# Where a block of fused linear attention and two expert layers begins and ends: tiles kept, units made and products ordered anew

## The chip, the cores and the metric

The kernel runs on one core of a Trainium2 chip. Its time is the device time of one execution in microseconds (us). A core has a matrix engine (TensorE, PE in the profile), a vector engine (VectorE, DVE), a scalar engine (ScalarE, ACT), a general engine (GpSimd, POOL) and a sync engine (SyncE, SP), which here issues nearly all loads and stores. Each engine runs its own instructions in the order in which the program gives them; semaphores tie the engines together.

## What is computed

Three layers follow one another; all are in float32.

```python
# 1: linear attention with decay, 4 batches, 8 heads, 768 steps, head size 64
state = gamma[None, :, None, None] * state + einsum('bhd,bhe->bhde', k[:, :, t], v[:, :, t])
y[:, :, t] = scale * einsum('bhd,bhde->bhe', q[:, :, t], state)
# 2: gated layer on x, 3072 tokens x 512, d_ff = 1536
x = ((x @ w_a) * (x @ w_b)) @ w_out
# 3: eight experts, each token goes to the one with the largest logit, F = 1024
e_idx = argmax(x @ w_gate, axis=1)
gate_w = softmax(x @ w_gate)[arange(N), e_idx]
eom = sigmoid(x @ w_output_gate)
for e in range(8):
    mask = e_idx == e
    out[mask] = gate_w[mask, None] * eom[mask, e, None] * (relu(x[mask] @ w1[e]) @ w2[e])
```

## The kernel before

**Matmuls.** Each float32 product is three matmuls: `mm3` (lines 111 to 113) multiplies high by high, high by low and low by high parts. A tile is therefore split: ACT makes the high part (a cast), DVE the low part (the difference). A split of a 128x1024 tile is `L687` on ACT and `L688` on DVE; `L682` makes the difference of two quarters of x ahead of a split (`less`).

**Blocks of tokens.** The 3072 tokens are worked in four blocks: block 0 and block 1 with 512 tokens, block 2 and block 3 with 1024. In each, d_ff is walked in 12 steps f of 128 columns. Blocks 0 and 1 do it plainly: `proj`, `gate` (rows `gs`, cast on ACT and subtracted on DVE, lines 581 and 584), and `down`, which multiplies the gated rows with a w_out tile `wos` into the four banks acc0 to acc3.

**Blocks of sums.** Blocks 2 and 3 use a scheme with seven products in place of eight (`block_of_sums`). x is split into quarters and sums of them: B21, B11, U1, U2, B22, U3, U4. The weights of a step come as two `unit` tiles, the first with four and the second with three combinations of weight quarters. A step is seven `product` calls of six matmuls each, into two banks by turns: p1 (`r`) and p0 (`q`). Between the products ACT and DVE copy, add and multiply the banks into `a1`, `b2` and `g2`. `a1` becomes the gated rows `gs` of half of the tokens, used in the next step's `down`; `g2` is kept in `later` tiles for the other half. In block 2 (`fresh`) the units are made on the go: `load_weights` and `sum_weights` (four POOL sums, line 645) and `make_unit`, which loads the quarters kept in memory (`q_d`), casts on ACT (line 656) and subtracts on DVE (line 657); `store_unit` writes them to `q_d`, and block 3 loads them back with `load_unit`.

**Deferred passes.** `later_pass` runs after each of these blocks ("2d" after block 2, "3d" after block 3). It walks f again and multiplies the kept rows (`later_split`: `gd`) with w_out into four more banks. Its w_out tiles are loaded anew: `passes` is the list of (pass, f) in order, and `next_wos` issues the next load into a ring of three buffers. `between` finishes the block's last `down` and copies its banks out (`evac_x2`, lines 604 and 606).

**What runs beside.** `spread` deals other work out over the slots of a block: the attention of block j+1, the routing (`route`), the splitting of x (`x_steps`, which returns a list in two parts), and the loads of the experts. Expert 0's first rows (`up2`, `down2`) start right behind pass 3d: they are gathered (POOL, line 848) by an index table that `route` writes to memory by scatter (line 415), and a last part of the routing (`todo`) is dealt out over their loop. `load_expert` splits an expert's weights (ACT line 462, DVE line 463) and loads the next.

**Buffers.** `room(i, ...)` hands out one of some fourteen large buffers by number; a tile that takes a number waits until the last tile there has been read to its end. SP issues its DMAs in the order of the program: one that must wait for a buffer holds up those behind it.

Of the kernel before, what the change touches and what calls it, by code (L numbers as in the profile page):

```python
# [34 lines left out]
LEAD = 256  # L35
# [17 lines left out]
def attention_moe_moe2(ctx: ExitStack, tc: tile.TileContext, a: dict, out: bass.AP):  # L53
# [243 lines left out]
    def route(i0, n, by_pe):  # L297
# [134 lines left out]
        if by_pe:  # L432
            out = [bank((s_t, 0))]
            for t in range(1, n):
                out.append(bank((s_t, t), (s_l, t - 1)))
            return out + [bank((s_l, n - 1)), s_m, bank((s_r,)), lambda: (s_e(), s_s())]
# [109 lines left out]
    passes = [(j, f) for j in (2, "2d", 3, "3d") for f in range(NF1)]  # L546
# [76 lines left out]
    UNIT_AT = [7, XH, XL]  # L623
# [12 lines left out]
    def load_weights(f):  # L636
        if f < NF1:
            w = raw_w[f] = room(10, [128, 8, 256], F32, "wsum")
# [8 lines left out]
    def make_unit(n):  # L647

        if n < 2 * NF1:
            f, h = divmod(n, 2)  # L650
            t = new_unit(2, n)
            k = 1 if h else 2
            q0 = UNIT_Q[h][0]
            sync.dma_start(f32(t[:, :k]), q_d[f][:, q0 : q0 + k])
# [19 lines left out]
    def x_steps(j):  # L674
# [9 lines left out]
        def split(eng, q):  # L684
# [13 lines left out]
            split(dve, "U2"),  # L698
            split(dve, "U3"),
            less(dve, "U4", "B21", "U2"),  # L700
            split(dve, "B22"),
# [17 lines left out]
    LATER_AT = [8, 9, 11]  # L719

    def block_of_sums(j, slot):
        fresh = j == 2
        for f in range(NF1):
            next_wos()
# [26 lines left out]
            if fresh:  # L751
                low0 = make_unit(2 * f + 2)
# [28 lines left out]
            gt[j, f] = gs  # L781
            if fresh:
# [4 lines left out]
        return gd0  # L787
# [7 lines left out]
    def later_pass(j, gd, slot, between):  # L795

        key = f"{j}d"
        nxt = None
        for f in range(NF1):
            if 0 < f < NF1 - 1:  # L800
                next_wos()
            w = wos[key, f]
            for i, tag in enumerate(("p1", "p0", "acc0", "acc1")):
                if f == 0 and i == 2:
                    between()
                if i == 2 and f + 1 < NF1:
                    nxt = later_split(f + 1)
                if f == 0:
                    accs[4 + i] = sum_bank(tag)
                c = slice(128 * i, 128 * i + 128)  # L810
                mm3(accs[4 + i], gd[:, 0, c], gd[:, 1, c], w[:, 0], w[:, 1], f == 0, f == NF1 - 1)
            wos.pop((key, f))
            gd = nxt
            slot()

# [61 lines left out]
    def up(p, f, d, c0, n):  # L877
        cc = slice(c0, c0 + n)
        for k in range(KD):
# [3 lines left out]
    def up2(f, d, c0, n, which=None):  # L883
        up(ph[f % 2 if which is None else which], f, d, c0, n)
# [9 lines left out]

# [441 lines left out]
```

## Time and profile before

| what | value |
|---|---|
| median of 3 runs | 1042.28 us (1037.99 to 1044.7) |
| the profiled execution | 1038.58 us |
| its span | 1036.8 us |
| mean granted clock of TensorE | 0.987 of full speed |
| TensorE (PE) | 94% busy, 7248 matmuls |
| VectorE (DVE), ScalarE (ACT), GpSimd (POOL) | 59%, 35%, 24% busy |
| moved by DMA | 222.30 MB, mean 214 GB/s |
| w_out tiles | 48 loads of 512 KB |
| first units of a step from `q_d` (block 3) | 12 loads of 1024 KB |

The span is what the profiler saw from the first to the last instruction; the execution's own time is 1.8 us longer. Times in the rows below count from the start of the span. "Busy" of PE includes matmuls that wait inside the pipeline, so a full share need not be full speed.

Block 1's last steps and block 2's first lie between 259 and 297.6 us, the rest of block 2 up to 455, pass 2d up to 495.7, block 3 up to 650.6, pass 3d with the start of expert 0 up to 705.5, and the loop over expert 0's first rows up to 744.2. The experts behind that are not touched.

### The profile page before, as it was taken

What the parts mean: (1) busy time and instruction counts of PE and PEld (TensorE: products, weight loads), DVE (VectorE), ACT (ScalarE), POOL (GpSimd) and SP (SyncE); (2) the same over time, 40 slices, a digit from 0 to 9 for tenths busy, and PEclk for the clock granted to TensorE, in tenths of its full rate; (3) what the DMA queues carried; (4) which work ended last, traced back from release to release, by engine and by line L of the source; (5) the groups of instructions that cost most, each with busy time, mean ns of one, the idle gap of its engine ahead of it and who ended that gap; (6) DMA issues with size and microseconds to landing.
All of it is one profiled execution on the core that took longest, in us unless ns stands there. A gap on an engine that the chain in (4) does not pass through costs nothing. (4 is left out here: it accounts for less than half of the span.)

```text
span 1036.8 us, 19417 instructions
## 1 busy us (share of the span) xinstructions
PE 975.3 (94%) x7248; PEld 795.3 (77%) x7249; DVE 607.6 (59%) x1213; ACT 361.1 (35%) x668; POOL 249.6 (24%) x238
## 2 busy tenths in 40 slices
PE   6899999999779999989999999888799999999997
PEld 5688888877557777767777777667698888889886
DVE  4899866877627676555576576343265444444541
ACT  3677742223312222233211112333154443344431
POOL 3211011225415443520012212220420220311211
PEclk9899999999989999999999999999999999999999
DMA  6999968767876876656966864752374653535620
GB/s 240 345 330 313 295 216 314 271 239 194 298 300 245 283 233 208 249 144 225 351 218 223 265 218 158 226 201 61 104 215 152 192 173 101 169 114 185 192 90 28
DMA packets 78549, 222.30 MB, mean 214 GB/s; under 512 B 13374, under 2 KB 22846, under 8 KB 76865
## 3 DMA queue, kind: packets, MB, share of 16 engines
q1 hardware_dynamic: 71136, 201.06, 58.5%
q0 software_dynamic: 6704, 18.93, 5.4%
q8 instruction: 82, 1.34, 0.5%
q10 hardware_dynamic: 576, 0.56, 0.2%
q14 instruction: 51, 0.41, 0.1%
HBM read 170.13 MB, written 51.30 MB: 214 GB/s over the span
## 5 line engine op out<-in xcount | busy, mean ns | idle before, releaser
L922 DVE TENSOR_TENSOR ew<-wraw,ew 128x512 fp32r<-128x512 f32 x112 | 76.4, 690 | 55.6 <-ACT ew L921 49.0
L342 DVE SCALAR_TENSOR_TENSOR junkd<-x2r,wcol 128x512 bf16<-128x512 f32 x128 | 104.5, 816 | 3.6 <-DMA x2r<-x_d 1.5
L888 DVE SCALAR_TENSOR_TENSOR hs<-ph,hs 128x384 fp32r<-128x384 f32 (+4 forms) x72 | 39.0, 542 | 113.1 <-ACT hs L887 90.1
L111 PE MATMUL ph<-xe,ew 128*128 128x384 f32 (+4 forms) x288 | 98.1, 341 | 2.8 <-DVE x L604 2.1
L112 PE MATMUL ph<-xe,ew 128*128 128x384 f32 (+4 forms) x288 | 95.2, 330 | 0.3 <-DVE xe L873 0.3
L113 PE MATMUL ph<-xe,ew 128*128 128x384 f32 (+4 forms) x288 | 95.2, 330 | 0.0
L921 ACT CAST ew<-wraw 128x512 fp32r<-128x512 f32 x112 | 68.1, 617 | 57.7 <-PE acc L113 43.8
L111 PE MATMUL acc<-ew,hs 128*128 128x512 f32 (+1 forms) x216 | 85.6, 396 | 1.0 <-ACT hs L887 0.6
L113 PE MATMUL acc<-ew,hs 128*128 128x512 f32 (+1 forms) x216 | 85.5, 396 | 0.0
L112 PE MATMUL acc<-ew,hs 128*128 128x512 f32 (+1 forms) x216 | 85.3, 395 | 0.0
L111 PE MATMUL acc<-wos,gs 128*128 128x512 f32 x192 | 78.4, 408 | 6.2 <-ACT gs L779 4.8
L908 POOL DMA_INDIRECT out<-y,idx x27 | 27.5, 1018 | 230.6 <-ACT y L907 148.0
L765 POOL TENSOR_TENSOR later<-later,b 128x512 f32<-128x512 f32 x24 | 38.3, 1595 | 181.0 <-DVE b L764 181.0
L111 PE MATMUL p<-xs,ar 128*128 128x512 f32 x192 | 77.7, 405 | 1.4 <-DVE z L253 1.4
L111 PE MATMUL p<-U,unit 128*128 128x512 f32 x192 | 76.4, 398 | 2.4 <-DVE b L764 1.9
L113 PE MATMUL acc<-wos,gs 128*128 128x512 f32 x192 | 77.2, 402 | 0.8 <-DVE gs L780 0.8
L887 ACT ACTIVATE hs<-ph 128x384 fp32r<-128x384 f32 (+4 forms) x72 | 34.6, 480 | 122.1 <-PE ph L113 94.5
L113 PE MATMUL p<-xs,ar 128*128 128x512 f32 x192 | 75.7, 394 | 0.1
L112 PE MATMUL p<-xs,ar 128*128 128x512 f32 x192 | 75.6, 394 | 0.0
L112 PE MATMUL acc<-wos,gs 128*128 128x512 f32 x192 | 75.0, 390 | 0.0
L113 PE MATMUL p<-U,unit 128*128 128x512 f32 x192 | 74.8, 390 | 0.0
L112 PE MATMUL p<-U,unit 128*128 128x512 f32 x192 | 74.8, 390 | 0.0
(193 smaller groups left out, 2154.3 us busy)
## 6 DMA issues: line engine op xcount, KB each, us to landing
wraw<-in_ex SPq DMA_DIRECT2D x64, 512.0 KB
wos<-wos_d SPq DMA_DIRECT2D x48, 512.0 KB
wide<-in_w_ab SPq DMA_DIRECT2D x24, 512.0 KB
q_d<-unit SPq DMA_DIRECT2D x24, 512.0 KB
unit<-q_d SPq DMA_DIRECT2D x12, 1024.0 KB
qk<-in_qk SPq DMA_DIRECT2D x23, 512.0 KB
vk<-in_vk SPq DMA_DIRECT2D x23, 512.0 KB
q_d<-ar SPq DMA_DIRECT2D x36, 256.0 KB
```

Source lines behind the costliest of these rows:

```text
L111: pe.matmul(outp, lhsT=wh, rhs=rh, start=start, stop=False, skip_group_check=more)
L112: pe.matmul(outp, lhsT=wh, rhs=rl, start=False, stop=False, skip_group_check=more)
L113: pe.matmul(outp, lhsT=wl, rhs=rh, start=False, stop=stop, skip_group_check=more)
L342: dve.scalar_tensor_tensor(junk, x, 1.0, y, op0=ALU.mult, op1=ALU.mult, accum_out=out)
L765: pool.tensor_tensor(g2, g2, b2, op=ALU.mult)
L887: act.activation(h[:, 0, :n], p[:, :n], AF.Relu)
L888: dve.scalar_tensor_tensor(h[:, 1, :n], p[:, :n], 0.0, f32(h[:, 0, :n]), op0=ALU.max, op1=ALU.subtract)
L908: st = pool.indirect_dma_start(out=out[:, :], out_offset=bass.IndirectOffsetOnAxis(ap=ix[:, 1:2], axis=0), in_=y, in_offset=None, bounds_c ...
L921: act.copy(ew[f][:, part, 0], t[:, part])
L922: dve.tensor_tensor(ew[f][:, part, 1], t[:, part], f32(ew[f][:, part, 0]), op=ALU.subtract)
```

## The change

Five things are changed.

1. *w_out.* The tiles of f = 9, 10, 11 stay on chip at the end of block 2 and block 3, and the deferred pass begins with them (`KEPT`, `LATER_ORDER`). Pass 2d ends with f = 0, 1, 2, and block 3 begins with those three. `passes` is shorter by nine loads. The pass writes to p1, p0, acc2, acc3, and `between` finishes the row groups 2, 3 before 0, 1. In a block's last step the groups 2 and 3 of f = 10 come behind U4, and the first `later_split` ahead of U4.
2. *Units.* A unit's load (`fetch_unit`) is apart from its making. Unit 0 is asked for two steps earlier, unit 1 one step, the weights of f = 0 half a step, and the quarters are stored two steps earlier (`keep_quarters(f + 2)`). In block 2 the fetches come right behind the copy of a1 and behind U2.
3. *Splits of x for block 2.* Three steps come behind gate 11, two behind `make_unit(1)`, and four in the first slots of block 2, where attention then starts four slots later. B22 is split ahead of U3. The units of block 3 are loaded within pass 2d.
4. *Order in a step.* Product B11 stands ahead of `down(j, f - 1, [0])`.
5. *Expert 0's first rows.* `up2` is cut in two halves, and the routing's steps come three to an f. Four of the eight `load_expert` go from pass 3d into the ends of that loop's steps; banks change names.

The core of the diff:

```diff
+    KEPT = [NF1 - 3, NF1 - 2, NF1 - 1]
+    LATER_ORDER = {2: [*KEPT, *range(3, NF1 - 3), 0, 1, 2], 3: [*KEPT, *range(NF1 - 3)]}
-    passes = [(j, f) for j in (2, "2d", 3, "3d") for f in range(NF1)]
+    passes = [(2, f) for f in range(NF1)] + [("2d", f) for f in LATER_ORDER[2][3:]]
+    passes += [(3, f) for f in range(3, NF1)] + [("3d", f) for f in LATER_ORDER[3][3:]]
...
-    UNIT_AT = [7, XH, XL]
+    UNIT_AT = [7, 8, XH]
...
+    def fetch_unit(n):
+        if n < 2 * NF1:
+            f, h = divmod(n, 2)
+            k = 1 if h else 2
+            q0 = UNIT_Q[h][0]
+            sync.dma_start(f32(new_unit(2, n)[:, :k]), q_d[f][:, q0 : q0 + k])
...
 (block_of_sums)
-            next_wos()
+            last = f == NF1 - 1
+            if not last and (fresh or f > 1):
+                next_wos()
...
             act.copy(a1, r)
             if fresh:
+                fetch_unit(2 * f + 2)
                 sum_weights(f + 1)
             slot()
+            product(q, u, 0, "B11", True)
+            dve.tensor_tensor(a1, a1, q, op=ALU.add)
             if f:
                 down(j, f - 1, [0])
-            product(q, u, 0, "B11", True)
-            dve.tensor_tensor(a1, a1, q, op=ALU.add)
...
             if fresh:
+                fetch_unit(2 * f + 3)
                 low0 = make_unit(2 * f + 2)
...
-            if f:
+            if f and not last:
                 down(j, f - 1, [2, 3])
-                wos.pop((j, f - 1))
-            if f == NF1 - 1:
-                next_wos()
-                gd0 = later_split(0)
+            if last:
+                gd = later_split(KEPT[0])
             product(q, u, 0, "U4", False)
...
+            if last:
+                down(j, f - 1, [2, 3])
...
 (later_pass)
-            if 0 < f < NF1 - 1:
+            if 0 < n < NF1 - 2:
                 next_wos()
...
 (block 1)
+                    if f == 9:
+                        fetch_unit(0)
+                    if f == 10:
+                        load_weights(0)
+                        fetch_unit(1)
                     load_wo(f + 1)
-                    keep_quarters(f)
+                    if f + 2 < NF1:
+                        keep_quarters(f + 2)
...
-                        make_unit(1)()
-                        load_weights(1)
+                        for s in x_rest[:3]:
+                            s()
...
+                        make_unit(1)()
+                        for s in x_rest[3:5]:
+                            s()
...
-        slot, flush = spread([(attention_steps(3), 0, 78), (route(4, 4, False), 2, 82)])
+        slot, flush = spread([(x_rest[5:], 0, 4), (attention_steps(3), 4, 78), (route(4, 4, False), 14, 82)])
...
-        loads = [lambda f=f: load_expert(f) for f in range(6)]
+        loads = [lambda f=f: load_expert(f) for f in range(4)]
...
 (loop over expert 0's first rows)
-                up2(f, xst(0), LEAD, LEAD)
+                up2(f, xst(0), LEAD, LEAD, ks=range(2))
+                next_todo()
+                up2(f, xst(0), LEAD, LEAD, ks=range(2, KD))
                 hs[f] = relu(f, LEAD)
-                if todo:
-                    todo.pop(0)()
+                next_todo()
...
+            load_expert(f + 4)
```

**DVE, from the last steps of block 1 into block 2.** A row is a line of the code, the operation, what it writes and reads, and the size; `U1` to `U4`, `B11`, `B22` are split tails of x, `xraw` rows are differences ahead of a split, `g_sb` and `gs` are the gate of block 1, `unit` is a unit's tail. Before:

```order
L688 TENSOR_TENSOR B11_3300<-xraw_2001,B11_3300 128x1024
L682 TENSOR_TENSOR xraw_2001<-xraw_2671,xraw_2001 128x1024
L682 TENSOR_TENSOR xraw_2671<-xraw_2671 128x1024
L576 TENSOR_TENSOR g_sb_3341<-p1_3328,a_sb_3322 128x512
L584 TENSOR_TENSOR gs_3343<-g_sb_3341,gs_3343 128x512
L688 TENSOR_TENSOR U1_3348<-xraw_2001,U1_3348 128x1024
L682 TENSOR_TENSOR xraw_2001<-xraw_2671,xraw_2001 128x1024
L688 TENSOR_TENSOR U2_3364<-xraw_2001,U2_3364 128x1024
L688 TENSOR_TENSOR U3_3392<-xraw_2671,U3_3392 128x1024
L576 TENSOR_TENSOR g_sb_3408<-p1_3395,a_sb_3384 128x512
L584 TENSOR_TENSOR gs_3410<-g_sb_3408,gs_3410 128x512
L657 TENSOR_TENSOR unit_3413<-wsum_3346,unit_3413 128x2x256
```

With the change, from behind the gate of f = 10 on (`x2` is a copy out of block 1's first bank):

```order
L665 TENSOR_TENSOR unit_3175<-wsum_3311,unit_3175 128x2x256
L579 TENSOR_TENSOR g_sb_3403<-p1_3390,a_sb_3383 128x512
L587 TENSOR_TENSOR gs_3405<-g_sb_3403,gs_3405 128x512
L690 TENSOR_TENSOR xraw_2007<-xraw_2677,xraw_2007 128x1024
L690 TENSOR_TENSOR xraw_2677<-xraw_2677 128x1024
L696 TENSOR_TENSOR U1_3412<-xraw_2007,U1_3412 128x1024
L665 TENSOR_TENSOR unit_3313<-wsum_3311,unit_3313 128x2x256
L690 TENSOR_TENSOR xraw_2007<-xraw_2677,xraw_2007 128x1024
L696 TENSOR_TENSOR U2_3430<-xraw_2007,U2_3430 128x1024
L607 COPY x2_3450<-acc0_2155 128x512
L696 TENSOR_TENSOR B22_3481<-xraw_2677,B22_3481 128x1024
```

The tails of U1, U2 and U3 stood among the last gates of block 1 and now stand behind the last gate (the `gs` row), with those of B22 and U4 among and behind them; the tail of unit 0 stands ahead of that gate.

**PE, one step of block 3.** `p1` and `p0` are the two banks, `acc0` the first row group of `down`; the rows left out are more matmuls of the product above them. Before:

```order
L113 MATMUL p0_6450<-U4_5538,unit_6402 128x512
...
L113 MATMUL p1_6542<-B21_5346,unit_6443 128x512
L111 MATMUL acc0_5666<-wos_6351,gs_6533 128x512
L112 MATMUL acc0_5666<-wos_6351,gs_6533 128x512
L113 MATMUL acc0_5666<-wos_6351,gs_6533 128x512
L111 MATMUL p0_6543<-B11_5366,unit_6443 128x512
...
L113 MATMUL p0_6543<-B11_5366,unit_6443 128x512
L111 MATMUL p1_6542<-U1_5422,unit_6443 128x512
```

With the change:

```order
L113 MATMUL p0_6434<-U4_5534,unit_6384 128x512
...
L113 MATMUL p1_6528<-B21_5338,unit_6427 128x512
L111 MATMUL p0_6529<-B11_5358,unit_6427 128x512
...
L113 MATMUL p0_6529<-B11_5358,unit_6427 128x512
L111 MATMUL acc0_5655<-wos_6335,gs_6519 128x512
L112 MATMUL acc0_5655<-wos_6335,gs_6519 128x512
L113 MATMUL acc0_5655<-wos_6335,gs_6519 128x512
L111 MATMUL p1_6528<-U1_5416,unit_6427 128x512
```

The six matmuls of B11 have moved from behind the three of `acc0` to the place ahead of them, right behind B21.

**SP's queue, from the end of block 2 through pass 2d.** `wos` is a w_out tile, `unit` a unit for block 3, `x_d<-x` a store of finished rows (three more of them where rows are left out). Before:

```order
L552 DMA wos<-wos_d 128x1024
L634 DMA unit<-q_d 128x2048
L552 DMA wos<-wos_d 128x1024
L610 DMA x_d<-x_5323 128x512
...
L552 DMA wos<-wos_d 128x1024 x10
L634 DMA unit<-q_d 128x1536
L634 DMA unit<-q_d 128x2048
L610 DMA x_d<-x_5557 128x512
```

With the change:

```order
L673 DMA q_d<-unit 128x1024 x2
L613 DMA x_d<-x_5315 128x512
...
L555 DMA wos<-wos_d 128x1024 x2
L637 DMA unit<-q_d 128x2048
L555 DMA wos<-wos_d 128x1024 x3
L637 DMA unit<-q_d 128x1536
L555 DMA wos<-wos_d 128x1024 x3
L637 DMA unit<-q_d 128x2048
L555 DMA wos<-wos_d 128x1024
L613 DMA x_d<-x_5549 128x512
```

Two w_out tiles and a unit stood ahead of the first stores and ten tiles behind them; now the stores come first, nine tiles follow, and three units stand among them.

## Rows read from the trace of the kernel before

**Rows 1.** The page, part 1: busy time, share of the span, instructions.
```profile
PE 975.3 (94%) x7248; PEld 795.3 (77%) x7249; DVE 607.6 (59%) x1213; ACT 361.1 (35%) x668; POOL 249.6 (24%) x238
```

**Rows 2.** Stretches (us): busy time and count per engine, PE clock, DMA share, GB/s.
```profile
259.00:297.60 38.60, 24.57 (x203) 17.68 (x202) 16.70 (x24) 10.89 (x19) 13.44 (x15) 0.87 0.89 326
297.60:455.00 157.40, 154.82 (x1423) 120.58 (x1422) 101.42 (x214) 40.33 (x79) 71.39 (x68) 1.00 0.67 229
455.00:495.70 40.70, 36.47 (x158) 28.91 (x157) 24.59 (x27) 16.28 (x23) 2.24 (x2) 1.00 0.72 232
495.70:650.60 154.90, 151.04 (x642) 117.52 (x641) 99.58 (x242) 29.11 (x53) 31.77 (x25) 1.00 0.68 231
650.60:705.50 54.90, 45.60 (x217) 35.81 (x216) 22.64 (x47) 19.78 (x35) 10.12 (x10) 0.97 0.68 212
705.50:744.20 38.70, 31.61 (x206) 27.84 (x206) 10.42 (x37) 9.13 (x23) 5.90 (x6) 0.96 0.23 63
```

**Rows 3.** PE's timeline, 290 to 293: start, length, instruction, [idle before <-releaser].
```profile
292.67 0.79 PE L111 MATMUL p<-B,unit 128*128 128x512 f32 x1 [10.50 <-DMA unit<-q_d]
```

**Rows 4.** DVE by line, 252 to 284: group | busy, mean ns | idle before.
```profile
L688 DVE TENSOR_TENSOR U<-xraw,U 128x1024 fp32r<-128x1024 f32 x4 | 5.2, 1295 | 1.8 <-ACT U L687 1.8
...
L682 DVE TENSOR_TENSOR xraw<-xraw 128x1024 f32<-128x1024 f32 x2 | 2.4, 1218 | 0.0
```

**Rows 5.** ACT by line, 252 to 284.
```profile
L687 ACT CAST U<-xraw 128x1024 fp32r<-128x1024 f32 x4 | 4.2, 1050 | 5.0 <-DVE xraw L682 5.0
```

**Rows 6.** DVE's timeline, 255 to 284.
```profile
262.85 0.69 DVE L584 TENSOR_TENSOR gs<-g_sb,gs 128x512 fp32r<-128x512 f32 x1 [0.68 <-ACT gs L581]
...
277.45 1.75 DVE L657 TENSOR_TENSOR unit<-wsum,unit 128x512 fp32r<-128x512 f32 x1
```

**Rows 7.** POOL by line, 252 to 284.
```profile
L645 POOL TENSOR_TENSOR wsum<-wsum 128x256 f32<-128x256 f32 x8 | 6.2, 792 | 10.8 <-DMA wsum<-wab_d 10.6
```

**Rows 8.** Stretches right behind two waits of PE, columns as in rows 2.
```profile
292.60:297.60 5.00, 4.93 (x15) 3.96 (x16) 0.00 (x0) 0.59 (x1) 1.57 (x3) 0.70 0.95 384
668.20:671.00 2.80, 2.72 (x7) 2.17 (x8) 0.00 (x0) 0.00 (x0) 0.00 (x0) 0.50 0.76 310
```

**Rows 9.** PE's timeline in a step of block 3.
```profile
597.63 0.39 PE L113 MATMUL p<-U,unit 128*128 128x512 f32 x1
...
598.99 0.39 PE L113 MATMUL p<-B,unit 128*128 128x512 f32 x1
599.70 0.50 PE L111 MATMUL acc<-wos,gs 128*128 128x512 f32 x1 [0.32 <-ACT gs L779]
...
600.76 0.39 PE L111 MATMUL p<-B,unit 128*128 128x512 f32 x1
```

**Rows 10.** All engines' timeline in the same step: ACT and DVE.
```profile
599.02 0.62 ACT L779 CAST gs<-a 128x512 fp32r<-128x512 f32 x1 [5.82 <-DVE a L777]
599.67 0.69 DVE L780 TENSOR_TENSOR gs<-a,gs 128x512 fp32r<-128x512 f32 x1 [0.68 <-ACT gs L779]
...
600.45 0.59 ACT L732 COPY a<-p 128x512 f32<-128x512 f32 x1 [0.81 <-DVE gs L780]
```

**Rows 11.** PE's waits in block 2's rest, then block 3: us, times, longest.
```profile
PE acc L111 <- ACT gs L779: 2.1, 4, 0.5
...
PE acc L111 <- ACT gs L779: 2.7, 7, 0.8
```

**Rows 12.** PE's waits in pass 2d, then pass 3d.
```profile
PE p L111 <- DMA wos<-wos_d: 3.6, 2, 2.7
...
PE p L111 <- DMA wos<-wos_d: 6.2, 3, 2.8
```

**Rows 13.** PE's waits from 705.5 to 744.2.
```profile
PE pg L870 <- DMA xg<-x_d,idx: 4.4, 1, 4.4
PE ph L111 <- DVE x L604: 2.1, 1, 2.1
```

**Rows 14.** POOL's timeline, 720 to 740: the last scatter of the table.
```profile
730.18 0.98 POOL L415 DMA_INDIRECT tab_d<-pay,si  x1 [0.30 <-issue]
```

More of the change, by code (lines that the diff above doesn't have):

```diff
@@ L435, in route @@
                 out.append(bank((s_t, t), (s_l, t - 1)))
-            return out + [bank((s_l, n - 1)), s_m, bank((s_r,)), lambda: (s_e(), s_s())]
+            return out + [bank((s_l, n - 1)), s_m, s_e, bank((s_r,)), s_s]
         out = [lambda: (s_w(), s_x()), s_w] + [none] * 6
@@ L650, in make_unit @@
             f, h = divmod(n, 2)
-            t = new_unit(2, n)
+            t = units[2, n]
             k = 1 if h else 2
-            q0 = UNIT_Q[h][0]
-            sync.dma_start(f32(t[:, :k]), q_d[f][:, q0 : q0 + k])
             w = raw_w[f][:, 6:8] if h else raw_w[f][:, 4:6]
@@ L698, in x_steps @@
             split(dve, "U2"),
+            split(dve, "B22"),
             split(dve, "U3"),
             less(dve, "U4", "B21", "U2"),
-            split(dve, "B22"),
             split(dve, "U4"),
@@ L786, in block_of_sums @@
             slot()
-        return gd0
+        return gd
     def later_split(f):
@@ L875, in attention_moe_moe2, with up, up2 @@
     ph = {}
-    def up(p, f, d, c0, n):
+    def up(p, f, d, c0, n, ks=range(KD)):
         cc = slice(c0, c0 + n)
-        for k in range(KD):
+        for k in ks:
             kk = slice(128 * k, 128 * k + 128)
             mm3(p[:, :n], ew[f][:, 0, 0, kk], ew[f][:, 0, 1, kk], d[0][:, k, cc], d[1][:, k, cc], k == 0, k == KD - 1)
-    def up2(f, d, c0, n, which=None):
-        up(ph[f % 2 if which is None else which], f, d, c0, n)
+    def up2(f, d, c0, n, which=None, ks=range(KD)):
+        up(ph[f % 2 if which is None else which], f, d, c0, n, ks)
     def relu_to(h, p, n):
@@ L893, in relu @@
         return h
+    ROWS_AT = ["acc2", "acc3", "p0", "p1"]
     def down2(f, h, rows, a0=0, t0=0):
@@ L897, in down2 @@
             if f == 0:
-                accs[t] = ps1.tile([128, 512], F32, tag=f"acc{a0 + t}", name=f"acc{a0 + t}")
+                accs[t] = sum_bank(ROWS_AT[a0 + t])
             tt = slice(128 * t, 128 * t + m)
@@ L968, in expert @@
             for t in (2, 3):
-                accs[t] = ps1.tile([128, 512], F32, tag=f"acc{t}", name=f"acc{t}")
+                accs[t] = sum_bank(ROWS_AT[t])
         def rest(f, n):
@@ L1147, in attention_moe_moe2 @@
                     split_wo(f)
-                    if f == NF1 - 1:
+                    if f == 10:
                         sum_weights(0)
+                    if last:
+                        make_unit(0)()
+                        store_unit(0)
                 slot()
@@ L1154, in attention_moe_moe2 @@
                 gate(j, f, ta, pb, n, 3 * f + 1 if f and j == 0 else None)
-                if j and f == NF1 - 2:
-                    load_weights(0)
-                if j and f == NF1 - 1:
-                    make_unit(0)()
-                    store_unit(0)
+                if j and last:
+                    load_weights(1)
                 slot()
-                if f == NF1 - 1:
+                if last:
+                    if j == 0:
+                        keep_quarters(0)
+                        keep_quarters(1)
                     flush()
@@ L1224, in attention_moe_moe2 @@
         evac_x2(2048, range(4, 8), (5, 7))
-        for f in range(6, NF2):
-            load_expert(f)
         for i in range(2):
-            ph[i] = ps1.tile([128, 512], F32, tag=f"p{i}", name=f"ph{i}")
+            ph[i] = sum_bank(f"acc{i}")
         hs = {}
-        todo = [*route(20, 4, True), count]
+        nothing = lambda: None
+        todo = route(20, 4, True)
+        todo = [*todo[:6], nothing, todo[6], nothing, *todo[7:], count]
         def after():
```

63 lines of the change are left out of this document (34 added, 29 removed).

## The prediction

> **What bounds the kernel now.** I read the busy shares first: TensorE (PE) works 975.3 of 1036.8 us [rows 1], so about 61 us are left in all, and only what shortens PE's idle time can pay. Then I cut the span at the places that the change touches [rows 2]. The reader is to see that PE idles (stretch less busy time) 14.0 us in the 38.6 where block 1 ends and block 2 begins, 2.6 in the rest of block 2, 4.2 in pass 2d, 3.9 in block 3, 9.3 in pass 3d, and 7.1 while expert 0's first rows run: some 41 us. The untouched last 292.6 us idle 6.6. More is hidden in "busy" time, since a matmul after a wait starts slowly.
>
> Next I asked what PE waits for in each stretch. At the start of block 2 it is a unit from memory, 10.50 us ahead of f=1's first product [rows 3]. In the blocks of sums it is ACT's cast of the gated rows [rows 11]. In the deferred passes it is w_out tiles, 3.6 and 6.2 us [rows 12]. In the row loop it is the gathered rows, 4.4 us, and a DVE copy, 2.1 [rows 13].
>
> One length serves as a ruler: a 128x512 matmul every 0.2267 us, the pace within a product (from 597.63 to 598.99 are six of them, 1.36 us [rows 9]). What a stretch would take at that pace, against what it took, is its true loss.
>
> **Block 1's end and block 2's first step (A).** The change fetches unit 0 two steps earlier, unit 1 one step and the first weights half a step earlier, and issues unit 2's fetch right after f=0's first product. In before, f=0 is done at 292.67 − 10.50 = 282.2 and PE then stands until unit 2 lands [rows 3]. Unit 2's fetch now goes out near 271 with about 3 MB in front of it; at the 384 GB/s that the wires carried just after that wait [rows 8] this is 8 us, so it lands near 279, ahead of need.
> Late next is DVE. The tail of gate 11 ended at 262.85 + 0.69 [rows 6], behind a split tail that now comes later, so I put it at 262.4. Between it and U4, DVE's queue holds four differences of 1.22 us, five split tails of 1.30 [rows 4], two unit tails of 0.68 or more and four operations of 0.69 (the length in rows 10): 4.9 + 6.5 + 1.4 + 2.8 = 15.6. Two of the tails wait for ACT's cast of a difference just made, 1.05 each [rows 5], and the last additions about 2 us for products. 262.4 + 15.6 + 2.1 + 2 = 282.1; with attention's masks between, 283. U4's six matmuls end f=0 at 284.4, later than the 282.2 of before. f=1 starts at 284.4 in place of 292.67: 8.3 us. Behind the old wait the clock was granted at 0.70 for 5 us [rows 8], so 1.5 more come back. Top: 9.8.
> Against it: the new chain leaves PE idle in shorter pieces, and behind a wait of 2.7 us for w_out the clock was 0.50 for 2.8 us [rows 8], a loss of 1.4 each time. And the next weights' four sums, 0.79 each on POOL [rows 7], now run beside this DVE chain; a unit tail beside POOL's work took 1.75 us [rows 6] where one alone takes 0.68. If all four sums push DVE, 3.2 us go. I take off a little over half of both: **7**, with bounds 2 and 9.8.
> The Trainium skill (SBUF — State Buffer, Who interferes with whom) says that a DVE instruction with two SBUF inputs contends with a GpSimd instruction that reads SBUF, and that whoever comes second is fully blocked. The trace agrees in that one row of 1.75. By the rule each of the four sums that meets a difference or a tail costs its whole length, so that A would be 6.6 before anything is said of the clock; it is part of the first rival's mechanism, and no bound here rests on it.
>
> **Block 3 (D) and the rest of block 2 (B): one swap.** In each step the first w_out group, which needs the cast rows of f−1, stood right behind product B21; now B11 stands between them. In block 3 the trace shows the price. B21's last matmul starts at 598.99, the w_out matmul at 599.70, 0.71 for 0.23; then three matmuls take 600.76 − 599.70 = 1.06 for 0.68, as the second half of the rows comes late too [rows 9]. That is 0.48 + 0.38 = 0.86 a step. Block 3 has 12 × 42 products and 11 × 12 w_out matmuls, 636 × 0.2267 = 144.2; it took 154.9 [rows 2]. Of the 10.7 lost, 11 × 0.86 = 9.5 are these, and some 1.1 lie in its first step.
> Does the wait go, or move? The cast runs from 599.02 for 0.62, the subtraction from 599.67 for 0.69 [rows 10]: all is there at 600.36. B21 ends its pace at 598.99 + 0.23 = 599.22 and B11 takes 1.36, so the w_out group is due at 600.58. It fits by 0.2. Then ACT copies a1 once the subtraction is done, from 600.45 for 0.59 [rows 10], and U1, which overwrites that bank, is due at 600.58 + 0.68 = 601.26, again 0.2 later. Where DVE is late by a routing dot, some tenths remain. D: top 9.4, **8.6**, low 5.
> In block 2 only 4 waits for the cast appear as against 7 [rows 11], because attention's matmuls fill some slots. With 5 to 7 steps × 0.86 it is 4.3 to 6, and a crowded DVE may keep half. B: **4.3**, 2 to 6.
>
> **Pass 2d (C) and pass 3d (E).** A pass has 144 matmuls, and 12 more finish its block's last step: 156 × 0.2267 = 35.4. Pass 2d took 40.7 [rows 2], so 5.3 are lost, 3.6 of them in two w_out waits [rows 12]. The passes now start with tiles that are still on chip (f = 9, 10, 11); nine loads of 512 KB fall away, and the first reloaded tile is needed three tiles later. The x stores and block 3's units stand in SP's queue ahead of some of them, hidden by the three tiles' 3 × 2.7 us of matmuls. That the last two w_out groups move behind U4 opens a wait of about 1 us between U3 and U4, which share a bank, and closes one of that size behind U4, where those groups now cover the cast: nothing net. C: **4**, 1 to 5.
> E: w_out 6.2 in three waits [rows 12]; 1.4 by the half clock behind the longest [rows 8]; 2.1 of the first rows' wait for a DVE copy out of their bank [rows 13], since they now use banks that are emptied at the pass's start; about 1 of smaller waits; 10.7 in all. Expert tiles (a cast of 1.05 each by the tiles of that size [rows 5], and a load each on SP) still stand between the w_out tiles, so 1 or so may stay: **9.5**, 6 to 12.
>
> **Expert 0's first rows (F).** Finer steps bring the last rows' routing 1 to 2 us forward. But four expert tiles move into this loop, each 1.05 on ACT and some 1.2 on DVE by the tiles of that size [rows 4, 5], ahead of the loop's own work there; and behind the last scatter, at 730.18 [rows 14], the index table's way through memory stays what it was, and so the 4.4 us wait for the gathered rows [rows 13]. **1**, 0 to 5.
>
> **The sum.** 7 + 4.3 + 8.6 + 4 + 9.5 + 1 = 34.4. The profiled execution took 1038.58, the median of the runs is 1042.28; 34.4 off gives 1004.2 and 1007.9. I take 1005, nearer to the profiled execution, since the lowest run (1037.99) is there too.
>
> **Rivals.**
> 1. Block 2's start eats its gain: DVE, with POOL beside it and a half clock behind each new idle piece. A falls to 2 and B to 2: 7.3 less, 1012. For it: 15.6 us of queue in a stretch of about 20. Against: PE asks for U3 and U4 last. Chance 0.2.
> 2. The w_out wait moves to the first reloaded tile, behind x stores, units or raw expert tiles on SP. C falls to 1 and E to 5: 7.5 less, 1012.5. For it: units of up to 1 MB stand ahead of tiles in one queue. Against: three tiles are in hand. 0.1.
> 3. Everything at its top, and the row loop gains too: 9.8 + 6 + 9.4 + 5 + 12 + 5 = 47, so 992. 0.07.
> 4. Slower: in block 2 the fetch of unit 2f+2 now comes on SP ahead of stores and tiles. If its buffer is still being read, SP stands, and with it attention's loads, the weights and w_out. It decides once each of 11 steps waits over (34.4 − 4.3) / 11 = 2.7 us. A whole 1 MB unit at block 2's 229 GB/s [rows 2] is 4.6 us: 11 × 4.6 = 50 lost against 30 gained, 1038.6 − 30 + 50 = 1059. Against: the buffer asked for held unit 2f−1, which PE last read in U4 of the step before, and the DMA share is 0.67 [rows 2]. 0.03.
>
> **How the numbers follow.** The forecast has 0.6, the rivals 0.2, 0.1, 0.07 and 0.03. The range of 8 in 10 runs from 993, just above rival 3, to 1019, rivals 1 and 2 together (1005 + 7.3 + 7.5). About 1%, 10 us, is what a measurement can tell here from no change. Only rival 4, or most terms failing at once, comes out there: faster 0.95, same 0.03, slower 0.02.
>
> **What would show it.** In the changed kernel's profile f=1's first product should start near 284.4 with no wait for a unit (A); the waits for the cast should be gone from block 3, which should take about 146 us (D); pass 2d should take about 36.5 and pass 3d about 45, without w_out waits (C, E); the wait for the gathered rows should still be there with some 4 us (F). I am wrong if DVE's queue and POOL's sums hold PE as long as the unit did, or if SP's one queue hands the w_out wait on.

## The result and the profile after

The changed kernel takes 1008.92 us, the median of four runs (1008.56 to 1011.78), against 1040.13 us for the kernel before: a ratio of 0.970, with a 95% interval of 0.966 to 0.975. 31 us are gone; 34.4 were forecast, to 1005.

The page's first part for the changed kernel, and below it the same stretches as in [rows 2], cut at its own marks (f=0's and f=1's first products in block 2, pass 2d, block 3, pass 3d, the row loop; columns as there):

```profile
PE 962.7 (96%) x7248; PEld 797.6 (79%) x7249; DVE 602.6 (60%) x1213; ACT 361.9 (36%) x668; POOL 249.9 (25%) x238
```

```profile
266.30:286.10 19.80, 13.08 (x100) 9.43 (x99) 14.47 (x19) 8.03 (x12) 5.98 (x5) 0.91 0.63 238
286.10:445.30 159.20, 156.84 (x1502) 124.92 (x1501) 101.80 (x219) 42.42 (x83) 77.79 (x74) 1.00 0.72 249
445.30:480.80 35.50, 35.50 (x158) 29.22 (x157) 23.45 (x26) 16.30 (x23) 1.13 (x1) 1.00 0.69 249
480.80:633.10 152.30, 147.61 (x641) 118.34 (x640) 97.70 (x243) 28.98 (x53) 31.09 (x26) 1.00 0.66 225
633.10:676.80 43.70, 42.50 (x218) 35.20 (x218) 19.68 (x43) 17.68 (x32) 9.21 (x9) 1.00 0.63 198
676.80:715.00 38.20, 31.15 (x204) 28.20 (x203) 13.43 (x39) 11.32 (x25) 6.72 (x6) 0.91 0.33 94
```

PE's waits in the changed kernel, for block 1's end with block 2's first step, block 3, pass 3d and the row loop (pass 2d has none):

```profile
PE p L111 <- ACT a L742: 3.6, 1, 3.6
PE p L111 <- issue: 2.7, 1, 2.7
PE p L111 <- DVE a L748: 0.4, 1, 0.4
...
PE p L111 <- DVE a L787: 2.0, 2, 1.3
PE p L111 <- DVE b L776: 1.9, 3, 0.8
PE p L111 <- ACT a L742: 0.6, 1, 0.6
...
PE p L111 <- DMA wos<-wos_d: 1.2, 1, 1.2
...
PE pg L887 <- DMA xg<-x_d,idx: 6.3, 1, 6.3
```

The wait for a unit [rows 3], the waits for the cast [rows 11] and most of those for w_out [rows 12] are gone. In their place PE waits for DVE and ACT (the 2.7 us of the row "issue" end at 284.63, ahead of U4, right behind DVE's addition at L776, which ends at 284.53). Set against the profile of before, from first matmul to first matmul of each stretch, the six terms of the sum came out as follows:

| stretch | before | after | gain | forecast |
|---|---|---|---|---|
| A: up to f=1's first product | 292.67 | 286.10 | 6.6 | 7 (2 to 9.8) |
| B: block 2 from there | 162.3 | 159.2 | 3.1 | 4.3 (2 to 6) |
| C: pass 2d | 40.7 | 35.5 | 5.3 | 4 (1 to 5) |
| D: block 3 | 154.9 | 152.4 | 2.5 | 8.6 (5 to 9.4) |
| E: pass 3d | 54.9 | 43.6 | 11.3 | 9.5 (6 to 12) |
| F: the rest, to the last matmul | 325.5 | 323.9 | 1.6 | 1 (0 to 5) |

So the sum holds to 4 us, but D falls far below its bounds, C comes out just above its own, and the other terms say only that time was saved, not by which edit. The cut and the forecast differ in one thing: A's top of 9.8 held 1.5 us of clock behind f=1's first product, which the table counts in B. So A gave somewhat more than was forecast for it, and B somewhat less. Which edit saved what, the experiments are to say.

### The profile page after: what moved, and what is told of

It reads as the page before. It is cut to its first block, busy times and chain, and to the rows that moved or that the text cites. A ratio compares the mean times of both kernels' runs of the same rounds, so it can differ in the third digit from the quotient of the medians.

```text
span 1006.5 us, 19402 instructions
## 1 busy us (share of the span) xinstructions
PE 962.7 (96%) x7248; PEld 797.6 (79%) x7249; DVE 602.6 (60%) x1213; ACT 361.9 (36%) x668; POOL 249.9 (25%) x238
## 5 line engine op out<-in xcount | busy, mean ns | idle before, releaser
L342 DVE SCALAR_TENSOR_TENSOR junkd<-x2r,wcol 128x512 bf16<-128x512 f32 x128 | 99.9, 780 | 2.4
L111 PE MATMUL acc<-xe,ew 128*128 128x384 f32 (+4 forms) x288 | 98.4, 342 | 0.6 <-issue 0.6
L905 DVE SCALAR_TENSOR_TENSOR hs<-acc,hs 128x384 fp32r<-128x384 f32 (+4 forms) x72 | 39.0, 542 | 98.4 <-ACT hs L904 98.4
L113 PE MATMUL acc<-xe,ew 128*128 128x384 f32 (+4 forms) x288 | 95.4, 331 | 0.0
L112 PE MATMUL acc<-xe,ew 128*128 128x384 f32 (+4 forms) x288 | 95.3, 331 | 0.0
L111 PE MATMUL p<-U,unit 128*128 128x512 f32 x192 | 78.1, 407 | 11.8 <-ACT a L742 4.2
L111 PE MATMUL acc<-wos,gs 128*128 128x512 f32 x192 | 75.8, 395 | 0.0
L113 PE MATMUL p<-U,unit 128*128 128x512 f32 x192 | 75.5, 393 | 0.0
L112 PE MATMUL p<-U,unit 128*128 128x512 f32 x192 | 75.4, 393 | 0.0
L904 ACT ACTIVATE hs<-acc 128x384 fp32r<-128x384 f32 (+4 forms) x72 | 34.4, 478 | 113.9 <-PE acc L113 113.7
L113 PE MATMUL acc<-wos,gs 128*128 128x512 f32 x192 | 74.9, 390 | 0.0
L112 PE MATMUL acc<-wos,gs 128*128 128x512 f32 x192 | 74.8, 390 | 0.0
L789 ACT CAST gs<-a 128x512 fp32r<-128x512 f32 x24 | 14.9, 621 | 138.2 <-DVE a L787 127.0
L111 PE MATMUL p<-B,unit 128*128 128x512 f32 x144 | 57.5, 399 | 2.0 <-DVE a L787 2.0
L111 PEld LDWEIGHTS acc<-xe,ew 128*128 128x128 f32 x288 | 54.6, 189 | 3.8 <-issue 1.0
```

What stands on the lines that cost most here:

```text
L111: pe.matmul(outp, lhsT=wh, rhs=rh, start=start, stop=False, skip_group_check=more)
L112: pe.matmul(outp, lhsT=wh, rhs=rl, start=False, stop=False, skip_group_check=more)
L113: pe.matmul(outp, lhsT=wl, rhs=rh, start=False, stop=stop, skip_group_check=more)
L342: dve.scalar_tensor_tensor(junk, x, 1.0, y, op0=ALU.mult, op1=ALU.mult, accum_out=out)
L789: act.copy(gs[:, 0], a1)
L904: act.activation(h[:, 0, :n], p[:, :n], AF.Relu)
```

## The experiments

Every set of kernels ran beside runs of the kernel before on the same chip. The ratios are to those runs (95% intervals about ±0.005); 0.001 is 1 us. The difference of two ratios is thus known to some 6 us: by the totals, of the kernels made from the changed one only swap_undone and best_two stand clear of it, and passes_undone just so. The stretches are those of one profiled execution each, cut as above. In kernels without an edit ahead of f=1 the stretch A lies between 284.9 and 287.1, so about 1 us can be told there.

| kernel | median us | ratio | A | B | C | D | E | F |
|---|---|---|---|---|---|---|---|---|
| the changed kernel | 1008.92 | 0.970 | 286.1 | 159.2 | 35.5 | 152.4 | 43.6 | 323.9 |
| swap_undone | 1025.21 | 0.984 | 284.9 | 165.1 | 35.5 | 162.2 | 42.3 | 323.4 |
| swap_alone | 1026.52 | 0.984 | 293.7 | 159.1 | 40.5 | 147.3 | 58.2 | 328.9 |
| last_down_back | 1013.07 | 0.972 | 285.9 | 160.0 | 38.0 | 152.1 | 43.8 | 324.8 |
| kept_undone | 1013.76 | 0.973 | 285.4 | 161.7 | 38.6 | 150.7 | 44.4 | 324.7 |
| experts_back | 1010.23 | 0.973 | 286.4 | 159.0 | 36.4 | 152.6 | 45.5 | 321.0 |
| passes_undone | 1020.54 | 0.977 | 286.2 | 161.5 | 39.3 | 151.1 | 49.6 | 325.2 |
| fetch_late | 1017.71 | 0.974 | 284.1 | 164.6 | 36.4 | 152.1 | 42.6 | 324.5 |
| route_early | 1005.83 | 0.967 | 287.1 | 158.8 | 35.5 | 151.8 | 43.7 | 322.3 |
| dots_apart | 1003.41 | 0.965 | 283.8 | 158.5 | 35.6 | 150.6 | 43.6 | 323.3 |
| start_eased | 1003.30 | 0.966 | 281.8 | 158.3 | 36.8 | 152.2 | 43.3 | 322.8 |
| combo | 1008.03 | 0.964 | 278.9 | 158.3 | 35.5 | 157.3 | 43.2 | 325.2 |
| best_two | 997.68 | 0.960 | 279.4 | 157.4 | 35.6 | 150.4 | 43.1 | 323.3 |

The profiled execution of swap_alone took 1035.21 us, 8.7 above that kernel's median; only its two blocks are read below.

**swap_undone and swap_alone: what is the swap worth?** The first takes the changed kernel and undoes the order of B11 and the first w_out group; the second puts that order alone into the kernel before.

```diff
 (swap_undone; swap_alone is the reverse, on the kernel before)
+            if f:
+                down(j, f - 1, [0])
             product(q, u, 0, "B11", True)
             dve.tensor_tensor(a1, a1, q, op=ALU.add)
-            if f:
-                down(j, f - 1, [0])
```

> The changed kernel with the first w_out group again ahead of product B11 in both blocks of sums. Theory 1, the forecast's size (0.86 us a step in block 3, 4.3 us in block 2): 12.9 us slower than the changed kernel, near 1022; block 3 longer by 8 to 9 us. Theory 2, as the two traces read: the swap is worth only the difference of the stretches, 3.1 us in block 2 and 2.5 in block 3, and some 1.2 more in each that the last step now spends between U3 and U4: 7 to 8 us slower, near 1016.5; block 3 longer by 3.5 to 4.5.

> The kernel before with nothing changed but product B11 ahead of the first w_out group. Theory 1: 12.9 us faster than before, near 1027. Theory 2: 7 to 8 us faster, near 1032.5, block 3 at about 151 instead of 154.9. A third reading: if the swap needs the other parts (less DVE work beside it), it gives under 3 us here.

Without the swap the changed kernel is 14.5 us slower by the ratios (0.984 against 0.970, some 6 us either way); alone, the swap takes about 16 off the kernel before (0.984, 5 either way). The forecast's 12.9 lies within both. My second theory, which read the swap's worth off the two traces, falls: it had block 3 at about 151 with the swap alone. Block 3 in swap_alone, then PE's waits there:

```profile
493.20:640.50 147.30, 145.76 (x642) 118.92 (x641) 98.87 (x242) 29.34 (x53) 31.39 (x25) 1.00 0.71 243
```

```profile
PE p L111 <- DVE b L764: 0.8, 1, 0.8
PE p L111 <- DVE a L777: 0.4, 1, 0.4
PE p L111 <- DVE a L737: 0.3, 1, 0.3
```

The reader is to see 147.3 against the 144.2 of pure pace, and no wait for the cast. Alone, the swap gave D 7.6 of the 8.6, inside its bounds: of the steps f=1 to 10, nine are 0.64 to 0.85 us shorter and one 1.26, where 0.86 was forecast, and the last is 0.45 longer. In block 2 it gave 3.2. That makes 10.8 in the two blocks; where the rest of the 16 lies, the trace does not show.

In the changed kernel block 3 takes 152.4: something else in the change costs 5.1 us there, and D in the table is the difference of the two. Without the swap the same cost is 7.3 (162.2 in swap_undone against 154.9). Of the 9.8 us that block 3 is longer in swap_undone, 4.5 lie in the one step f=6, where DVE, then PE show:

```profile
565.50 0.69 DVE L342 SCALAR_TENSOR_TENSOR junkd<-x2r,wx 128x512 bf16<-128x512 f32 x1 [1.55 <-DMA wx<-in_wog,ix]
566.12 0.08 DVE L342 DVE_READ_ACCUMULATOR junkd<-x2r,wx 128x1 f32 x1
566.12 0.68 DVE L787 TENSOR_TENSOR a<-a,p 128x512 f32<-128x512 f32 x1
```

```profile
567.51 0.50 PE L111 MATMUL acc<-wos,gs 128*128 128x512 f32 x1 [3.39 <-ACT gs L789]
```

L342 is a dot of the routing: a row of x times a row of weights, multiplied and summed by DVE; here the weights are gathered output-gate rows. It waits for its gather, the multiplication behind it comes late, and with it the cast and the w_out group. So the 9.8 hold more than the price of 0.86 a step.

**route_early and dots_apart: what takes D back?** The change deals block 3's routing from slot 6 instead of slot 1. One kernel puts slot 1 back; the other leaves slot 6 and puts more empty steps between a gather of output-gate rows and the dots that need it.

```diff
 (route_early)
-[*route(8, 4, False), *route(12, 4, False)], 6, 82)
+[*route(8, 4, False), *route(12, 4, False)], 1, 82)
 (dots_apart)
-        out += [lambda: (s_m(), s_g(0), s_g(1)), none, none, none]
+        out += [lambda: (s_m(), s_g(0), s_g(1))] + [none] * 7
...
-                out += [none, none]
+                out += [none] * (7 if t == 1 else 2)
```

> The changed kernel with block 3's routing dealt out from slot 1 to 82 again, not from 6 to 82. Theory: the swap is worth 7.6 us in block 3 by itself (154.9 to 147.3), and the changed kernel keeps only 2.5 of it because the denser routing puts two dots on DVE ahead of an operation that PE waits for; with the old spread block 3 falls from 152.4 to 149 or less, the whole to about 1005.5. Rival: the loss comes from the last step's new order and from loads; block 3 stays within 1 us of 152.4.

> The changed kernel with four more empty steps between the gathers of the output-gate rows and the first dot on them, and five more behind the second, so that DVE stands less behind a gather that has not landed. Theory: in the changed kernel such a dot holds DVE in block 3's last step and in step 6, where product B11 now waits for DVE's multiplication (1.3 and 0.7 us); without it block 3 is 2 to 3 us shorter, the whole near 1006. Rival: the denser dealing that follows puts more dots in other slots and takes it back; within 1 us of 1009.

route_early is 3 us faster by the ratio, within the intervals, and shortened block 3 by 0.6 us only, so by that number the rival held. Its steps tell more. Steps f=1 to 10 of block 3 took 126.6 us in the changed kernel, 123.6 here and 122.9 in swap_alone: the denser dealing did cost 3 us. They are lost again in the last step, which took 17.6 instead of 15.2. DVE there, in route_early's timeline, and PE behind it:

```profile
618.00 0.69 DVE L342 SCALAR_TENSOR_TENSOR junkd<-x2r,wx 128x512 bf16<-128x512 f32 x1 [1.50 <-DMA wx<-in_wog,ix]
618.62 0.08 DVE L342 DVE_READ_ACCUMULATOR junkd<-x2r,wx 128x1 f32 x1
618.62 0.68 DVE L787 TENSOR_TENSOR a<-a,p 128x512 f32<-128x512 f32 x1
```

```profile
619.36 0.79 PE L111 MATMUL p<-B,unit 128*128 128x512 f32 x1 [2.27 <-DVE a L787]
```

A dot waits for its gathered row, the multiplication that empties bank p0 stands behind it in DVE's queue, and product B11, which now comes right behind B21, waits for that bank. The changed kernel has the same picture in its last step, PE's 1.30 us wait at 620.81:

```profile
619.45 0.69 DVE L342 SCALAR_TENSOR_TENSOR junkd<-x2r,wx 128x512 bf16<-128x512 f32 x1 [3.23 <-DMA wx<-in_wog,ix]
...
620.07 0.68 DVE L787 TENSOR_TENSOR a<-a,p 128x512 f32<-128x512 f32 x1
...
620.81 0.50 PE L111 MATMUL p<-B,unit 128*128 128x512 f32 x1 [1.30 <-DVE a L787]
```

dots_apart removes that wait: the last step falls from 15.2 to 13.6 and block 3 to 150.6, 1.8 us shorter, a little under the theory's 2 to 3. By the ratios it is 5.7 us faster than the changed kernel, about as much as two ratios can tell apart; 2.3 of these come ahead of f=1. The routing dealt out in block 1 has the same new empty steps, but that they gave the 2.3 is not shown.

**start_eased: what bounds A now?** The difference and the split of U2 go from block 1's last step into block 2's first slots, and attention starts two slots later.

```diff
                         make_unit(1)()
-                        for s in x_rest[3:5]:
-                            s()
...
-spread([(x_rest[5:], 0, 4), (attention_steps(3), 4, 78), (route(4, 4, False), 14, 82)])
+spread([(x_rest[3:], 0, 4), (attention_steps(3), 6, 78), (route(4, 4, False), 14, 82)])
```

> The changed kernel with the difference and split of U2 moved from block 1's last step into block 2's first slots, and attention starting two slots later there. Theory: PE's 3.65 us wait for the copy of a1 is ACT's queue, which held that copy behind the cast of U2 and the cast behind a DVE difference; and the masks of attention stand ahead of the addition that U4 needs. f=0 of block 2 should fall from 19.8 to about 17 us, the whole to 1006. Rival: DVE's list is the bound however it is dealt; PE waits as long ahead of U2 and U4, f=0 stays at 19 to 20.

f=1 starts at 281.8 instead of 286.1, f=0 takes 17.4 us, and the whole is 4.8 us faster by the ratios. The changed kernel's timeline shows why, on DVE, on ACT and on PE:

```profile
268.03 1.76 DVE L690 TENSOR_TENSOR xraw<-xraw 128x1024 f32<-128x1024 f32 x1
...
269.82 1.04 ACT L695 CAST U<-xraw 128x1024 fp32r<-128x1024 f32 x1 [3.65 <-DVE xraw L690]
270.77 1.55 ACT L609 COPY x<-acc 128x512 f32<-128x512 f32 x3
272.20 0.61 ACT L742 COPY a<-p 128x512 f32<-128x512 f32 x1
...
272.86 0.50 PE L111 MATMUL p<-U,unit 128*128 128x512 f32 x1 [3.65 <-ACT a L742]
```

The copy of a1, which frees the bank for U1, stood on ACT behind a cast that waited 3.65 us for a DVE difference, and behind three copies of finished rows. With the cast behind the copy, PE starts U1 without a wait; what is left is a shorter wait ahead of U2, for DVE's addition of B11:

```profile
270.99 0.76 PE L111 MATMUL p<-U,unit 128*128 128x512 f32 x1 [2.37 <-DVE a L748]
```

The wait ahead of U4 stays, 2.26 us for 2.69. The forecast had ACT's casts in DVE's chain, but not this copy behind one of them.

**fetch_late: is it the fetch's place?** All of A stays, but unit 2f+2 is fetched behind U2 and unit 2f+3 behind B22's addition, where they are made.

```diff
-                fetch_unit(2 * f + 2)
                 sum_weights(f + 1)
...
-                fetch_unit(2 * f + 3)
+                fetch_unit(2 * f + 2)
                 low0 = make_unit(2 * f + 2)
...
                 low0()
+                fetch_unit(2 * f + 3)
```

> The changed kernel with block 2's unit fetches issued where the unit is made again (behind U2 and behind the addition after B22), all else as changed. Theory: the fetch's place is what took the 10.5 us wait away; asked for near 278, with a w_out tile and attention's loads in front, unit 2 lands 3 to 8 us later, so f=1's first product waits up to 4 us, and later steps little: 2 to 5 us slower, 1012. Rival: the stores of quarters, moved out of the way, were enough; no wait for a unit, 1009 within 1 us.

4 us slower by the ratio, within the intervals, as the theory had it, but not where it had it. f=1 starts at 284.1 with no wait for a unit; block 2 is 5.4 us longer, with one wait, that of this line, at the start of f=3, a step that then took 16.7 us for 15.0:

```profile
315.53 0.75 PE L111 MATMUL p<-B,unit 128*128 128x512 f32 x1 [2.81 <-DMA unit<-q_d]
```

So the 10.50 us of [rows 3] had gone with the rest of A. The earlier stores and the earlier first units are the parts that bear on this load; they were not tried apart. The new place of the later fetches keeps a smaller wait from coming up two steps on.

**kept_undone, experts_back, passes_undone: what freed the passes?** One kernel loads all twelve w_out tiles in every pass, one puts expert 0's tiles 4 to 7 back into and behind pass 3d, one does both and asks for block 3's units ahead of and behind pass 2d, as before.

```diff
 (kept_undone)
+    passes = [(j, f) for j in (2, "2d", 3, "3d") for f in range(NF1)]
...
-                gd = later_split(KEPT[0])
+                gd = later_split(0)
...
-        order = LATER_ORDER[j]
-        for f in KEPT:
-            wos[key, f] = wos[j, f]
+        order = range(NF1)
...
 (experts_back)
-        loads = [lambda f=f: load_expert(f) for f in range(4)]
+        loads = [lambda f=f: load_expert(f) for f in range(6)]
...
-            load_expert(f + 4)
 (passes_undone: both, and)
+        load_unit(3, 0)
...
         later_pass(2, gd, slot, lambda: between(2, 1024))
         flush()
+        load_unit(3, 1)
+        load_unit(3, 2)
```

> The changed kernel with every pass loading all its twelve w_out tiles in order 0 to 11, as before. Theory: keeping three tiles is what removed the w_out waits, so that 3.6 us in pass 2d and 6.2 us in pass 3d come back and the half clock behind the longest with 1.4: 10 to 11 us slower, near 1019.5. Rival: the waits had come from what else stood in the sync queue and on ACT (units, expert tiles), which stays changed here: only 2 to 4 us slower, near 1012.

> The changed kernel with expert 0's tiles 4 and 5 again split and loaded within pass 3d and 6 and 7 behind it, none in the row loop. Theory: those tiles stood between the w_out tiles on the sync queue and held expert 0's first rows at the end; pass 3d grows from 43.6 to 47 to 49 us, the rows behind it gain 1 to 2, in all 2 to 4 us slower, 1012. Rival: tiles kept on chip removed the waits alone; pass 3d at 44.5, the row loop 1 to 2 us shorter, total 1008.5.

> The changed kernel with all that bears on the queue of the passes undone together: every pass loads twelve w_out tiles, expert tiles 4 to 7 are back in and behind pass 3d, and the units of block 3 are asked for ahead of and behind pass 2d. Undone alone, the kept tiles cost 3.1 and 0.8 us in the two passes and the experts 1.9 in the second. Theory: each part alone already frees the queue, so alone they show little; together the waits for w_out come back, pass 2d at about 40 and pass 3d at 50 or more, 1020. Rival: the parts add up: 38.6 and 46.3, 1014.

PE's waits in kept_undone (pass 2d, then 3d), and in passes_undone:

```profile
PE p L111 <- ACT gd L801: 1.6, 2, 0.8
PE p L111 <- DMA wos<-wos_d: 0.5, 2, 0.4
...
PE p L111 <- DMA wos<-wos_d: 1.7, 2, 0.9
```

```profile
PE p L111 <- DMA wos<-wos_d: 2.3, 2, 1.4
PE p L111 <- ACT gd L801: 0.8, 1, 0.8
...
PE p L111 <- DMA wos<-wos_d: 3.9, 3, 2.7
PE p L111 <- ACT gd L801: 0.8, 1, 0.8
```

My theory on kept_undone falls: it is 2 to 5 us slower, not 10. The waits for w_out are 0.5 us in pass 2d (none in the changed kernel, 3.6 before) and 1.7 in pass 3d (1.2 and 6.2). More of pass 2d's 3.1 us is a wait of 1.6 for ACT's cast of the kept rows. Block 2 is 2.5 us longer and block 3 1.7 shorter, its last step 13.6 us for 15.2, which no theory had. experts_back costs 1.9 us in pass 3d (45.5, between the theory's 47 and the rival's 44.5) and gives 2.9 back in the row loop, where the wait for gathered rows falls from 6.3 to 3.3 us; in all it is 1 to 3 us slower, within the intervals. Together they cost more than their sum: pass 3d grows by 6.0, where 0.8 and 1.9 were the parts, and the waits are 3.9. Either edit by itself keeps most of the waits away from pass 3d; the two replace each other. That they do it by freeing SP's queue is the theory, and the waits for w_out agree with it. In pass 2d, 39.3 against 38.6, the units' place adds little. Pass 3d lies at the theory's 50, pass 2d between theory and rival; the total is 7.4 us slower by the ratio, 11.6 by the medians.

**last_down_back: is the last step's order worth anything?** The last two w_out groups of f = 10 go back ahead of U4.

```diff
-            if f and not last:
+            if f:
                 down(j, f - 1, [2, 3])
...
-            if last:
-                down(j, f - 1, [2, 3])
```

> The changed kernel with the last two w_out groups of f = 10 again ahead of U4 in the last step of each block. Theory 2: in the changed kernel about 1.2 us of waiting moved from the pass into the block; put back, blocks 2 and 3 are shorter by 0.8 to 1.2 us each, passes 2d and 3d longer by as much, total 1009 within 1 us. Rival: the new place gains by itself, and the passes' gains of 5.3 and 11.3 rest on it in part: 2 to 3 us slower, 1011.5.

The last steps of blocks 2 and 3 are 1.1 and 1.0 us shorter, pass 2d is 2.5 longer, pass 3d 0.2. By the ratio it is 1.4 us slower, within its interval: the order moves some 1 us from a pass into its block, and no more than that can be told.

**combo and best_two: a faster version.** combo joins start_eased, dots_apart and route_early; best_two leaves route_early out.

> The changed kernel with the eased start of block 2, the gathers further from their dots, and block 3's routing dealt from slot 1 again. Theory: the three lie in different places and add: 2.4 us at the start, 4 to 5 in block 3 (152.4 to 147.5), 999 to 1001 in all. Rival: more empty steps in the same slots make the dealing denser, so that DVE is late at other products; block 3 stays at 150, no better than 1003.

> The changed kernel with the eased start of block 2 and the gathers further from their dots, and block 3's routing dealt from slot 6 as in the change. Theory: what spoiled the three together was one slot of block 3, where a dot that waits for rows of x held DVE ahead of the addition that U4 needs (4.1 us); with slot 6 the dealing is the one that gave block 3 150.6 us, and the start 17 us: about 8 us under the changed kernel, 1000 to 1002. Rival: the gains do not add, since steps beyond the start only wait elsewhere; no better than 1003.

combo kept its start (278.9), but block 3 took 157.3, with a wait of 4.09 us for DVE in step 6. There a dot waited for rows of x, ahead of the addition that U4 needs:

```profile
560.49 0.69 DVE L342 SCALAR_TENSOR_TENSOR junkd<-x2r,wcol 128x512 bf16<-128x512 f32 x1 [2.88 <-DMA x2r<-x_d]
561.11 0.08 DVE L342 DVE_READ_ACCUMULATOR junkd<-x2r,wcol 128x1 f32 x1
561.11 0.68 DVE L776 TENSOR_TENSOR b<-b,p 128x512 f32<-128x512 f32 x1
```

best_two takes 997.68 us (996.9 to 998.27), a ratio of 0.960 (0.958 to 0.963): 10 us faster than the changed kernel, and a little faster than the theory's 1000. Block 2 from f=1, and block 3 in it:

```profile
279.30:436.80 157.50, 156.24 (x1506) 125.29 (x1502) 104.76 (x223) 42.19 (x83) 77.64 (x73) 1.00 0.74 256
472.30:622.80 150.50, 146.99 (x642) 118.47 (x641) 99.18 (x243) 29.26 (x53) 30.88 (x26) 1.00 0.68 228
```

## Why the prediction was right, point by point

- **A (7; measured 6.6).** The unit wait went, DVE's queue came next, and f=1 started 1.7 us later than the worked 284.4: the last gate's tail ended at 263.4, not 262.4, and a difference beside POOL took 1.76 us for 1.22. What PE waited for first was ACT's copy, which the working had not in it. So the size was near, in part by luck: the bottom of the chain was not the one that was summed. fetch_late corrects the reason too: at f=1 the wait stayed away without unit 2's early fetch, with which the working had removed it.
- **B and D (12.9 for the swap; measured 10.8 alone, 15.7 undone, in the two blocks).** Mechanism and price were right: swap_alone shows the price step by step, and swap_undone adds one step with a long wait for a dot. That B and D together show 5.6 in the table is the step that failed: the working took the rest of the two blocks to stay as it was. "Where DVE is late by a routing dot, some tenths remain" was far too small. In block 3 ten steps lost 3.7 us against swap_alone, 3.0 of them by the dealing from slot 6, and the last step 1.4. dots_apart, which leaves that step's new order and takes the dot's wait away, has it at 13.6, so the 1.4 was that wait.
- **C and E (13.5; measured 16.6).** The size was near, the cause was not. Keeping three tiles is worth 2 to 5 us; fewer other loads in the queue of pass 3d do as much, and with both undone, and the units moved, 7 to 12 us return. About 5 us of pass 3d's gain (54.9 against 49.6) stay even then. The 2.1 us wait of the first rows for a copy out of their bank [rows 13] is gone, and the waits for w_out are still 2.3 us less (3.9 for 6.2); the banks were not tried alone, and what the rest is stays open. The 1.4 us for "the half clock behind the longest" wait were misread: the half clock stood behind 2.67 us, and behind the longest, 2.77 at 693.12, the clock was 1.00 (last part).
- **F (1; measured 1.6).** The last scatter comes 22 us into the loop instead of 25, and the wait for the gathered rows grew from 4.4 to 6.3, not stayed. experts_back shows the price of the expert tiles in the loop, 2.9 us.
- **Rivals.** The first is half true: DVE, ACT and POOL took a few us at block 2's start (start_eased gives 4.3 back), and half the clock came once, not behind every idle piece: 0.62 of full from 272.8 to 275.6, behind 3.65 us, and 1.00 behind the 2.69 us wait that ended at 284.63. The second shows as one wait of 1.2 us in pass 3d. The slower one left no trace: without a wait for a unit in block 2, SP's order did no harm.
- **The sum (34.4; measured 30.4 by the stretches).** That it held to 4 us is in part luck: D gave 6.1 less than forecast and B 1.2, while C and E gave 3.1 more, for reasons that were not the forecast's.

## What to carry to other kernels

When an edit moves a consumer ahead, list what stands in front of its new producer on that engine's queue: with B11 right behind B21, a dot that waits for a gather cost 1.3 us in the changed kernel and 2.3 in route_early; in the old order too, one cost 3.4 where the dealing put it ahead of the multiplication (swap_undone). Price each edit with the others of the same stretch in place, and test it both alone on the old kernel and undone on the new one; for the same two blocks the difference of two traces gave the swap 5.6 us where the tests gave 10.8 and 15.7. Two edits that free one queue replace each other, so undoing either alone shows neither's worth.

## What the runs showed of the hardware

- A POOL sum of 128x256 took 0.79 us in [rows 7], and a DVE difference of 128x1024 1.22 [rows 4]. Where the two met in the changed kernel, a difference took 1.76 us (at 268.03), 0.5 more, and the four sums from 266.49 on 4.57 us, 1.4 more than four times 0.79. The Trainium skill (SBUF — State Buffer, Who interferes with whom) has a DVE instruction with two SBUF inputs contend with a GpSimd instruction that reads SBUF, and gives the shared ports to whichever issued first for its whole length, while the other blocks. The trace agrees that they contend. The working let each sum cost DVE its whole 0.79; the difference lost some 0.5, which would fit a wait for a sum already under way. Whether it was that, the trace does not show, since the four sums stand in one row. That A came out at 6.6, the number worked out from whole lengths, has other causes (above).
- Waits of the same length need not cost the same afterwards. Before, behind 2.67 us that ended at 668.28 the clock was 0.50, its lower level [rows 8]; behind 2.69 us (to 467.22) and 2.77 us (to 693.12) it was 1.00:

```profile
467.20:468.70 1.50, 1.48 (x7) 1.25 (x8) 0.00 (x0) 0.00 (x0) 0.00 (x0) 1.00 1.05 411
693.10:694.60 1.50, 1.48 (x7) 1.24 (x8) 0.00 (x0) 0.00 (x0) 1.14 (x2) 1.00 0.97 360
```

  In the changed kernel it was 0.62, a mix of the two levels, behind 3.65 us and 1.00 behind 2.69:

```profile
272.80:275.60 2.80, 2.42 (x6) 1.42 (x6) 1.81 (x3) 2.12 (x4) 0.00 (x0) 0.62 0.76 285
284.60:286.10 1.50, 1.47 (x7) 1.24 (x8) 0.53 (x1) 0.00 (x0) 1.50 (x1) 1.00 0.14 55
```

- DVE waited 4.9 us in all for gathers of output-gate rows in block 3 before, and 10.1 after. In the changed kernel the raw tiles of expert 0 are asked for at 613.10, beside the last step's gathers at 613.04; before, at 649.77, behind the last w_out loads. The dot started 6.4 us after the first gather began. In kept_undone and passes_undone, where the raw tiles come later again, it was 4.7 and 5.2 us, and the last step took 13.6 and 13.9 us for 15.2. But in dots_apart, where these gathers go out 7 us ahead of the raw tiles, it was 6.6 all the same. So the raw tiles are not the whole cause, and what slows the gathers stays open.
